# A decay attention and two MLPs on one core: the loads of queries and keys split into 104 and 24 rows, and the whole tokens rebuilt later

## The chip, the core and the metric

The kernel runs on one core of a Trainium2 chip. A core has a matrix engine (TensorE, PE in the profile, with its weight loads as PEld), a vector engine (DVE), a scalar engine (ACT), a general engine (GpSimd, POOL) and a queue engine (SyncE, SP) that here only issues DMA transfers. Each engine runs its own instructions in the order in which they stand and waits on semaphores for the others. The metric is device time in microseconds (us) of one execution.

## The reference

Two batches of eight heads of a decaying linear attention over 768 positions in blocks of 64, then two MLPs, all in float32:

```
rel   = pos[:, None] - pos[None, :]
Dmask = where(rel >= 0, lam ** rel, 0)
for b in range(12):                        # blocks of 64 positions
    intra = ((qb @ kb.T) * Dmask) @ vb
    inter = (qb * lam ** (pos + 1)) @ kv_state
    out[block b] = intra + inter
    kv_state = lam ** 64 * kv_state + (kb * lam ** (63 - pos)).T @ vb
x = out as [1536 tokens, 512]
h = x @ w_in;   x = (h * clip(h + 3, 0, 6) / 6) @ w_out        # first MLP, 2048 wide
h = x @ w_in2;  out = max(0.01 * h, h) @ w_out2                # second MLP
```

## The kernel before

**Attention.** The twelve blocks are the twelve chunks `c` = 0 to 11, both batches and all heads at once. Each chunk has three pieces on PE, 16 small float32 products each: the scores `s` (PSUM tile `pair`, from queries and keys), the state `t` (PSUM tile `a`, from the decayed keys `kd` and the values `vs`) and the output `o` (PSUM tile `h`, from the masked scores `r` and `vs`). Around them ACT copies the queries into `pair` (line 312), so that the state's share comes out of the same products; DVE masks the scores (`r`, line 320); POOL decays the keys (`kd`, line 294); ACT copies the state into the next chunk's `vs` (line 334). The output `o` is the MLP's input: ACT writes its high part `xh` (line 351), DVE the rest `xl` (line 349), and for chunks 0 to 7 ACT also copies the whole value out into `x_spare` (`att_spare`, line 362).

**Loads.** SP issues them in the order of the table `LOAD_ORDER`: a chunk's queries and keys are three loads of 128 rows of 2 KB (`load_qk`, into a ring of four places in `sums`), the values of two chunks two such loads (`load_v`, into `vs`), and two weight slices stand among them (`raw`, two loads each). The helper `load` (line 154) issues them all. Eight semaphores, `DMAHW0` to `DMAHW7`, go round: a load waits until the one eight before it has landed. The other half of a chunk's values is then copied within `vs` by `part_v` (line 287): ACT for chunks 0 to 2, DVE for 3 to 11.

**Borders.** `mm` counts the instruction records that PE gets (four for a float32 product, two for others). The first product at or past record 193 + 256 n + 8 is border n. From the sixteenth load on, six loads at a time wait for a border, through a dependency that `load` adds and that the table `AT_BORDER` repeats for the planner.

**Order.** Nothing is scheduled by hand. Class `Order` plays all operations through a model with a due time and a cost for each, and the order in which they start there is the order of the instructions. `LATENCY`, the costs in the `add` calls and the pieces that wait for a load set it. A change of one number can therefore move instructions on all engines.

**MLPs.** Weights come as 64-bit numbers and are composed to float32 on ACT and DVE (lines 428 to 461: `c`, `t`, `wh`, `wl`), four DVE operations and three ACT ones for a slice and one DVE operation for its low part. Blocks 0 and 1 of the first MLP (four slices of width, three groups of tokens each) use plain products, with a gate on ACT and DVE for each (`u`, `Gh`, `Gl`). From block 2 on, two token groups and two slices are multiplied by seven products instead of eight; these need sums of weights (`s`, line 484) and differences of tokens, T1 to T4, made from `x_spare` (`x_diff`, line 682) and split into high and low parts (line 688 on DVE). `sums_1` orders that work.

```
def load(out, in_):
    i = nc.sync.dma_start(out=out, in_=in_)
    k = (len(loads) - FIRST_LOADS) // LOADS_PER_BLOCK
    loads.append(i)
    if 0 <= k < len(AT_BORDER):
        tc.add_manual_dep(i.ins, borders[...].name, ..., reason="behind the border")
```

Of the kernel before, what the change touches and what calls it, by code (L numbers as in the profile page):

```python
# [9 lines left out]
F32 = mybir.dt.float32  # L10
# [10 lines left out]
DM = H * D  # L21
# [21 lines left out]
FIRST_BORDER, BLOCK, PAST_BORDER = 193, 256, 8  # L43
FIRST_LOADS, LOADS_PER_BLOCK = 15, 6
AT_BORDER = (('o', 0), ('s', 2), ('t', 3), ('s', 5), ('s', 6), ('s', 8), ('o', 8), ('s', 10))
LOAD_ORDER = (('qk', 0), ('v', 0), ('qk', 1), ('qk', 2), ('v', 2), ('qk', 3), ('qk', 4), ('v', 4), ('qk', 5), ('qk', 6), ('v', 6), ('qk', 7), (0, 0, 0), ('qk', 8), ('v', 8), ('qk', 9), ('qk', 10), ('v', 10), (0, 0, 1), ('qk', 11))
# [75 lines left out]
def decay_attention_two_mlps(ctx: ExitStack, tc: tile.TileContext, qkk, vv, lam, w1, w2, out):  # L122
    nc = tc.nc
    eng = {"act": nc.scalar, "dve": nc.vector, "pool": nc.gpsimd}

    sizes = {"raw": 3, "cv": 3, "cl": 2, "w0": 4, "w1": 5, "st": 2, "s": 2, "G": 3, "u": 3, "h": 2, "a": 2, "r": 3, "vs": 3}
    late = {"Gx": 3, "ux": 3}
    const = ctx.enter_context(tc.tile_pool(name="const", bufs=1))
# [23 lines left out]

    def load(out, in_):
        i = nc.sync.dma_start(out=out, in_=in_)  # L154
        k = (len(loads) - FIRST_LOADS) // LOADS_PER_BLOCK
        loads.append(i)
        if 0 <= k < len(AT_BORDER):
            tc.add_manual_dep(i.ins, borders[min(k, len(borders) - 1)].name, mybir.DependencyInfo(
                mybir.DependencyClass.Sync, mybir.DependencyReason.DATA), reason="behind the border")

# [98 lines left out]
    op_warm = add(("pe", T_WARM / 2), lambda _: dense(N_WARM - N_WARM // 2), -800, after=[op_lam])  # L259
    op_a = add(("dve", 1.5), consts_a, -100, takes=["u"] * 3 + ["r"])  # L260
    op_steps = add(("dve", 1.25), consts_b, -100, after=[op_lam, op_a], frees=["h"])
# [5 lines left out]
    def load_qk(c):  # L267
        def fn(_):
            for i in range(3):
                load(QK[c % NQ][:, i], qkk[c, :, i])  # L270
        return fn

    def load_v(c):

        def fn(_):
            vp = new("vs", [P, 2, 2, H, D], F32)
            VS[c], VS[c + 1] = vp[:, 0], vp[:, 1]
            for i in range(2):
                load(vp[:, i, 0], vv[c + i])
            if c == 0:  # L280
                nc.gpsimd.memset(vp[other[1], 0, 1], 0.0)
        return fn
# [70 lines left out]

    SPARE = {}

    def att_spare(c):
        def fn(_):
            j, i = divmod(c, SPT)
            if not i:
                SPARE[j] = pool["s"].tile([P, 2, 2, TT], F32, tag="s", name="x_spare")  # L360
            x = SPARE[j].rearrange("p j k (c b i) -> p (j k) c b i", c=SPT, b=2)[:, :, i]
            nc.scalar.copy(out=x, in_=PA["o", c])
        return fn

    x_ready, spared = {}, {}
    ld = {}
    for c in range(NSC):
        d = due_c[c] - 2.0
        ld["qk", c] = add(("dma", 2.05), load_qk(c), d, takes=["q"])
        ld["vp", c] = ld["vp", c - 1] if c % 2 else add(("dma", 1.4), load_v(c), d if c else 0.0, after=[ld["qk", c]], takes=["vs"])  # L370
        ld["v", c] = add(("act", 0.6 if c else 1.2) if c < 3 else ("dve", 0.5), part_v(c), d - 1.0, after=[ld["vp", c]])
    pieces = {}
    st, copies, masks, dense_ops, att_ops = {}, {-1: []}, [], [op_warm], []
    for c in range(NSC):
        d, last = due_c[c], c + 1 == NSC
        ks = [] if last else [add(("pool", 1.05), k_decay(c, b), d,
                                  after=[ld["qk", c], op_scan[b], st.get(c - 2)]) for b in ((1, 0) if c else (0, 1))]
# [3 lines left out]
        m = add(("dve", 1.13), mask(c), d + 1.2, after=[s, qc, op_const], takes=["r"] if c else [], frees=["pair"])  # L381
        masks.append(m)
        if c < 2:
            op_rows[1 - c] = add(("dve", 1.4), decay_rows(1 - c), d + 4.0, after=[m])
# [12 lines left out]
        x_ready[c] = add(("dve", 0.69), att_x(c, True), d + 5.0, after=[hi])  # L397
        if c < 2 * SPT:
            spared[c] = add(("act", 0.58), att_spare(c), d + 5.0, after=[hi], takes=["s"] * (not c % SPT))
        add(("none", 0.0), nothing, after=[x_ready[c], spared.get(c)], frees=["h"])  # L400
        att_ops += [x_ready[c], m, o, *ks, *copies.get(c, []), *([st[c]] if c in st else [])]
# [13 lines left out]
    def load_w(h):  # L415
        def fn(_):
            l, f, j = h
            RAW[h] = new("raw", [P, DM, 2], U32)
            raw, w = RAW[h].rearrange("p n t -> p (n t)"), (w1, w2)[l][f, j].bitcast(U32)
            for a in (slice(0, DM), slice(DM, 2 * DM)) if l + f < 2 else (slice(0, 2 * DM),):  # L420
                (load if h in LOAD_ORDER else nc.sync.dma_start)(raw[:, a], w[:, a])
        return fn
# [63 lines left out]

    composed, low = {}, {}
    for l in range(2):
        for f in range(NF):
# [11 lines left out]
            if paired(l, f) and f % 2:  # L501
                p, i = f // 2, None
                for n in range(4):
                    i = add(("dve", 0.43), w_sum(l, p, n), after=[composed[l, f - 1, 0], composed[l, f, 0], i])
                hi = add(("act", 1.05), s_high(l, p), after=[i], takes=["s"])
                s_ready[l, p] = add(("dve", 1.22), s_low(l, p), after=[hi], frees=["raw"])
                add(("none", 0.0), nothing, after=[i, low[l, f - 1, 0], low[l, f, 0]], frees=["cv"] * 2)
# [144 lines left out]

    XT, CS = {}, {}
    A_B = (("A11", "B11"), ("S1", "T1"), ("S2", "T2"), ("A12", "B21"), ("S3", "T3"), ("S4", "B22"), ("A22", "T4"))
# [22 lines left out]
    def spare(k, n):  # L677
        i = {"B11": 0, "T1": 0, "B21": 1, "T4": 1, "B12": 2, "T3": 2, "B22": 3, "T2": 3}[n]
        return SPARE[i // 2][:, i % 2]

# [3 lines left out]
    def x_split(k, n, lo, src):  # L684
        def fn(_):
            xh, xl = XT[k, n]
            if lo:
                nc.vector.tensor_tensor(out=xl, in0=src(k, n), in1=xh.bitcast(F32), op=ALU.subtract)
            else:
                nc.scalar.copy(out=xh, in_=src(k, n))  # L690
        return fn

# [280 lines left out]

    def sums_1():
        u = ("dve", 1.22)
        for n, t in (("B11", 0), ("B21", 0), ("B22", 1)):
            x_op[0, 0, n] = x_of(PAIR[t])
        t1 = add(u, x_diff(0, "T1", "B12", "B11", spare), after=list(spared.values()))
        t3 = add(u, x_diff(0, "T3", "B22", "B12", spare), after=[t1])
        t2 = add(u, x_diff(0, "T2", "B22", "T1", spare), after=[t3])  # L980
        t4 = add(u, x_diff(0, "T4", "B21", "T2", spare), after=[t2])
        for n, after in (("T1", [t2]), ("T2", [t4]), ("T4", [t4]), ("T3", [t3, last1[0, PAIR[1]]])):
            splits(0, 0, n, [op_late, *after], spare)
        done = [x_op[0, 0, n][0] for n in ("T1", "T4", "T3", "T2")]
        for d in (done[:2], done[2:]):
            add(("none", 0.0), nothing, after=d, frees=["s"])
# [72 lines left out]

    sums_1()  # L1060
    for b in range(SINGLE, len(BLOCKS[0])):
# [45 lines left out]
```

## Time and profile before

| | us |
|---|---|
| median of 3 runs | 563.14 |
| lowest and highest of them | 562.85, 564.15 |
| the profiled execution, whole time | 563.63 |
| its span, first to last instruction | 561.9 |
| PE busy | 548.5 (98% of the span) |
| DVE busy | 411.9 |
| ACT busy | 362.3 |

The span is what the profile shows; 1.7 us of the profiled execution's time lie around it. Matmuls are pipelined, so a busy PE may still be late. Idle time of an engine matters only where the last one to finish waits for it.

### The profile page before, as it was taken

What the parts mean: (1) busy time and instruction counts of PE and PEld (TensorE: products, weight loads), DVE (VectorE), ACT (ScalarE), POOL (GpSimd) and SP (SyncE); (2) the same over time, 40 slices, a digit from 0 to 9 for tenths busy, and PEclk for the clock granted to TensorE, in tenths of its full rate; (3) what the DMA queues carried; (4) which work ended last, traced back from release to release, by engine and by line L of the source; (5) the groups of instructions that cost most, each with busy time, mean ns of one, the idle gap of its engine ahead of it and who ended that gap; (6) DMA issues with size and microseconds to landing.
All of it is one profiled execution on the core that took longest, in us unless ns stands there. A gap on an engine that the chain in (4) does not pass through costs nothing.

```text
span 561.9 us, 9098 instructions
## 1 busy us (share of the span) xinstructions
PE 548.5 (98%) x3512; PEld 458.2 (82%) x3512; DVE 411.9 (73%) x690; ACT 362.3 (64%) x634; POOL 67.5 (12%) x77
## 2 busy tenths in 40 slices
PE   8888999999999999999999999999999999999996
PEld 5877888888788888888888888888888888888885
DVE  7879999987987974787689897686368943782342
ACT  5988895667666745578676886687268825683220
POOL 7651001101111101101000000000110110110000
PEclk9999999999999999999999999999999999999999
DMA  8984334534447433534200402241434622512332
GB/s 312 315 296 172 113 112 94 128 116 113 86 109 190 115 84 75 130 114 93 76 1 1 157 31 80 71 150 38 94 81 124 168 56 43 132 42 50 75 73 77
DMA packets 25596, 61.66 MB, mean 110 GB/s; under 512 B 3026, under 2 KB 3282, under 8 KB 25554
## 3 DMA queue, kind: packets, MB, share of 16 engines
q1 hardware_dynamic: 18672, 48.77, 26.8%
q0 software_dynamic: 6480, 11.80, 12.3%
q8 instruction: 27, 0.44, 0.4%
q10 hardware_dynamic: 402, 0.52, 0.3%
q14 instruction: 15, 0.12, 0.1%
HBM read 46.14 MB, written 3.15 MB: 88 GB/s over the span
## 4 chain that ended last, share of the span: by engine, by line
PE 90%; DVE 4%; DMA 2%; ACT 1%; issue 1%; POOL 1%; SPq 0%; DVEq 0%; POOLq 0%; ACTq 0%
PE acc L148 44%; PE h L148 27%; PE a L148 18%; DMA sums<-st 1%; DVE r L320 1%; DMA vs<-vv 1%; PE pair L148 1%; POOL kd L294 1%; DVE vs L287 1%; DVE t L441 0%; DVE u L550 0%; DVE t L451 0%; SPq L154 0%; DVE decay L242 0%; DVE Gl L563 0%
## 5 line engine op out<-in xcount | busy, mean ns | idle before, releaser
L580 POOL DMA_DIRECT2D sums<-st x45 | 39.5, 926 | 426.0 <-ACT st L636 426.0
L148 PE MATMUL acc<-Gl,wh 128*128 128x512 f32 x136 | 53.1, 390 | 0.1
L148 PE MATMUL acc<-Gh,wh 128*128 128x512 f32 x136 | 53.1, 390 | 0.0
L148 PE MATMUL acc<-Gh,wl 128*128 128x512 f32 x136 | 53.0, 390 | 0.0
L148 PE MATMUL acc<-wl,Gh 128*128 128x512 f32 (+1 forms) x128 | 49.6, 388 | 0.0
L148 PE MATMUL acc<-wh,Gh 128*128 128x512 f32 (+1 forms) x128 | 49.6, 387 | 0.0
L148 PE MATMUL acc<-wh,Gl 128*128 128x512 f32 (+1 forms) x128 | 49.5, 387 | 0.0
L451 DVE CUSTOM_DVE_ANT_0 t<-t,c 128x1024 uint16<-128x1024 uint16 x64 | 45.0, 704 | 2.2
L636 ACT COPY st<-acc 128x512 f32<-128x512 f32 x43 | 25.1, 587 | 32.1 <-PE acc L148 15.9
L428 ACT ACTIVATE c<-raw 128x512 uint32<-128x512 uint32 x64 | 42.7, 669 | 4.7 <-DVE t L451 3.1
L449 DVE SCALAR_TENSOR_TENSOR t<-raw,t 128x512 uint32<-128x512 uint32 x64 | 44.1, 688 | 1.1
L457 ACT CAST wh<-t 128x512 fp32r<-128x512 f32 (+1 forms) x64 | 37.7, 593 | 9.1 <-DVE t L451 6.2
L432 ACT ACTIVATE t<-raw 128x512 f32<-128x512 f32 x64 | 42.6, 667 | 0.0
L461 DVE TENSOR_TENSOR wl<-t,wh 128x512 fp32r<-128x512 f32 (+1 forms) x64 | 41.2, 652 | 0.7 <-ACT wh L457 0.4
L148 PE MATMUL a<-xh,wh 128*128 128x512 f32 (+1 forms) x108 | 38.9, 360 | 0.0
L566 DVE TENSOR_TENSOR Gl<-u,Gh 128x512 fp32r<-128x512 f32 x32 | 22.1, 689 | 22.9 <-ACT Gh L754 22.7
L148 PE MATMUL h<-xh,s 128*128 128x512 f32 x112 | 38.7, 390 | 0.0
L148 PE MATMUL a<-xh,wl 128*128 128x512 f32 (+1 forms) x108 | 38.7, 358 | 0.0
L148 PE MATMUL a<-xl,wh 128*128 128x512 f32 (+1 forms) x108 | 38.7, 358 | 0.0
L638 DVE TENSOR_TENSOR sums<-acc,sums 128x512 f32<-128x512 f32 x26 | 17.9, 690 | 28.0 <-PE acc L148 28.0
L438 DVE TENSOR_SCALAR t<-t 128x512 f32<-128x512 f32 x64 | 27.0, 422 | 15.3 <-ACT t L432 15.2
L760 ACT ACTIVATE u<-a 128x512 f32<-128x512 f32 x24 | 14.3, 597 | 25.8 <-PE a L148 25.8
(176 smaller groups left out, 1447.2 us busy)
## 6 DMA issues: line engine op xcount, KB each, us to landing
raw<-w SPq DMA_DIRECT2D x58, 512.0 KB, 3.3
sums<-st POOLq DMA_DIRECT2D x45, 256.0 KB, 4.1
sums<-qkk SPq DMA_DIRECT2D x36, 256.0 KB, 4.9
vs<-vv SPq DMA_DIRECT2D x12, 256.0 KB, 5.1
raw<-w SPq DMA_DIRECT2D x12, 256.0 KB, 4.1
out<-sums SPq DMA_DIRECT2D x19, 128.0 KB, 2.3
out<-sums ACTq DMA_DIRECT2D x3, 128.0 KB, 2.7
out<-sums SPq DMA_DIRECT2D x2, 64.0 KB, 2.3
```

The lines of the kernel that those rows point to most:

```text
L148: i = nc.tensor.matmul(out, a, x, **flags)
L428: nc.scalar.activation(out=CV[h][1], in_=RAW[h][:, :, 0], func=AF.Copy, scale=2.0 ** -29)
L432: return lambda _: nc.scalar.activation(out=CV[h][0].bitcast(F32), in_=RAW[h][:, :, 1].bitcast(F32), func=AF.Abs)
L438: nc.vector.tensor_scalar(out=t.bitcast(F32), in0=t.bitcast(F32), scalar1=MAG_MIN, scalar2=MAG_MAX, op0=ALU.max, op1=ALU.min)
L449: nc.vector.scalar_tensor_tensor(out=t, in0=RAW[h][:, :, 1], scalar=0xC0000000, in1=t, op0=ALU.bitwise_and, op1=ALU.bitwise_or)
L451: nc.vector.tensor_tensor(out=t, in0=t, in1=c, op=ALU.add)
L457: nc.scalar.copy(out=W[h][0][:, cols(*h)], in_=CV[h][0].bitcast(F32)[:, cols(*h)])
L461: return lambda e: eng[e].tensor_tensor(out=W[h][1][:, cols(*h)], in0=CV[h][0].bitcast(F32)[:, cols(*h)], in1=W[h][0].bitcast(F32)[:, cols ...
L566: nc.vector.tensor_tensor(out=gl, in0=U[s], in1=gh.bitcast(F32), op=ALU.subtract)
L580: return lambda _: nc.gpsimd.dma_start(out=SUM[t][:, e, :], in_=STAGE[t, e], accum_op=ALU.add)
L636: nc.scalar.copy(out=STAGE[t, e], in_=ps)
L638: nc.vector.tensor_tensor(out=acc, in0=ps, in1=acc, op=ALU.add)
```

## The change

All queries' and keys' loads from chunk 3 on are issued as two loads, of rows 0 to 103 and of rows 104 to 127; values and weights stay at 128 rows. `FIRST_LOADS` is 99, more than there are loads in the table, so no load waits for a border. Within a chunk the second and third load change places: the keys for `kd` come before the keys for the scores. `part_v` goes to ACT for the odd chunks from 3 on. `att_spare` is gone; instead `x_whole` adds `xh` and `xl` on DVE, four operations of 128x1024, once the attention is done, and `s` takes the attention's memory. Some costs and the DMA latency of the planner have other numbers, so that the order moves everywhere until about a third of the way through the program.

```diff
-LATENCY = {"dma": 2.0, "pe": 0.15, "act": 0.15, "dve": 0.15, "pool": 0.15}
+LATENCY = {"dma": 2.5, "pe": 0.15, "act": 0.15, "dve": 0.15, "pool": 0.15}
-FIRST_LOADS, LOADS_PER_BLOCK = 15, 6
+FIRST_LOADS, LOADS_PER_BLOCK = 99, 6
+FEWER = (slice(0, 104), slice(104, 128))
+FEWER_FROM, FEWER_QK, FEWER_V, FEWER_RAW = 3, (0, 1, 2), (), ()
-    def load(out, in_):
-        i = nc.sync.dma_start(out=out, in_=in_)
+    def load(out, in_, fewer=False):
         k = (len(loads) - FIRST_LOADS) // LOADS_PER_BLOCK
-        loads.append(i)
-        if 0 <= k < len(AT_BORDER):
+        loads.append(k)
+        for p in FEWER if fewer else (slice(0, P),):
+            i = nc.sync.dma_start(out=out[p], in_=in_[p])
+            if 0 <= k < len(AT_BORDER):
...
-            for i in range(3):
-                load(QK[c % NQ][:, i], qkk[c, :, i])
+            for i in (0, 2, 1):
+                load(QK[c % NQ][:, i], qkk[c, :, i], c >= FEWER_FROM and i in FEWER_QK)
...
-        ld["v", c] = add(("act", 0.6 if c else 1.2) if c < 3 else ("dve", 0.5), ...)
+        ld["v", c] = add(("act", 0.6 if c else 1.2) if c < 3 else ("act", 0.6) if c % 2 else ("dve", 0.8), ...)
...
-        if c < 2 * SPT:
-            spared[c] = add(("act", 0.58), att_spare(c), d + 5.0, after=[hi], takes=["s"] * (not c % SPT))
...
+    def x_whole(k, n):
+        def fn(_):
+            if n == "B11" or n == "B22" and not k:
+                SPARE[k, int(n == "B22")] = pool["s"].tile([P, 2 << k, 2, TT >> k], F32, ...)
+            x = [part([x[i].bitcast(F32) for x in X], k, n) for i in range(2)]
+            nc.vector.tensor_tensor(out=spare(k, n), in0=x[0], in1=x[1], op=ALU.add)
+        return fn
...
+        for n, t in (("B11", 0), ("B12", 1), ("B22", 1), ("B21", 0)):
+            w[n] = last_whole[0] = add(u, x_whole(k, n), after=[op_late, last_whole.get(0), *x_of(ts[t])],
+                                       takes=["s"] * (n == "B11" or n == "B22" and not k))
```

How the change moves instructions is shown at three places. First SP: `sums` is the ring of queries and keys, `vs` the values. From the third load of chunk 3 to the values of chunk 5 there stood before:

```order
L154 DMA sums<-qkk 128x512 [waits DMAHW0_49,PE_49]
L154 DMA sums<-qkk 128x512 [waits DMAHW1_49]
L154 DMA sums<-qkk 128x512 [waits DMAHW2_49]
L154 DMA sums<-qkk 128x512 [waits DMAHW3_49,Pool_49]
L154 DMA vs<-vv 128x512 [waits DMAHW4_49]
L154 DMA vs<-vv 128x512 [waits DMAHW5_49]
```

Now, chunk 4 and the values of chunks 4 and 5:

```order
L159 DMA sums<-qkk 104x512 [waits DMAHW4_49,PE_49]
L159 DMA sums<-qkk 24x512 [waits DMAHW5_49]
L159 DMA sums<-qkk 104x512 [waits DMAHW6_49,Pool_49]
L159 DMA sums<-qkk 24x512 [waits DMAHW7_49]
L159 DMA sums<-qkk 104x512 [waits DMAHW0_49]
L159 DMA sums<-qkk 24x512 [waits DMAHW1_49]
L159 DMA vs<-vv 128x512 [waits DMAHW2_49]
L159 DMA vs<-vv 128x512 [waits DMAHW3_49]
```

A chunk's three loads are six issues, each with its turn of the eight semaphores; the wait for PE at the third load of chunk 3 was a border, the one left is the ring's place coming free.

Second DVE, the masks and the copies of values in the middle of the attention (`pair` and `r` are scores before and after the mask, `xl0` the low part of the output for the first group of tokens). Before:

```order
L287 COPY vs_319<-vs_319 64x512 x2
L320 TENSOR_TENSOR r_414<-pair_364,decay_106 128x1024
L349 TENSOR_TENSOR xl0_111<-h_397,xh0_110 128x4x128
L349 TENSOR_TENSOR xl0_111<-h_436,xh0_110 128x4x128
L320 TENSOR_TENSOR r_502<-pair_394,decay_106 128x1024
L287 COPY vs_453<-vs_453 64x512 x2
L320 TENSOR_TENSOR r_549<-pair_499,decay_106 128x1024
```

Now, from the copy for chunk 8 to the first weight slice (`t_613`):

```order
L290 COPY vs_563<-vs_563 64x512
L352 TENSOR_TENSOR xl1_110<-h_616,xh1_109 128x4x128
L323 TENSOR_TENSOR r_682<-pair_584,decay_103 128x1024
L430 TENSOR_SCALAR t_613<-t_613 128x512
L433 TENSOR_SCALAR t_613<-t_613 128x512
L441 SCALAR_TENSOR_TENSOR t_613<-raw_491,t_613 128x512
L443 ISA t_613<-t_613,c_614 128x1024
```

Two copies in a row ahead of a mask have become one; the copy for chunk 8 now stands ahead of the mask of chunk 7 and of the first weight slice.

Third PE, the last pieces ahead of the first weight product (`pair` are scores, `a` states, `h` with `r` outputs, `h` with `wh` the MLP). Before:

```order
L148 MATMUL pair_659<-sums_109 64x64 x16
L148 MATMUL a_709<-vs_453,kd1_108 64x64 x16
L148 MATMUL h_735<-r_684,vs_453 64x64 x16
L148 MATMUL a_764<-vs_574,kd0_107 64x64 x16
L148 MATMUL h_789<-r_732,vs_574 64x64 x16
L148 MATMUL pair_785<-sums_109 64x64 x16
L148 MATMUL a_839<-vs_574,kd1_108 64x64 x16
L148 MATMUL h_861<-xh0_110,wh_811 128x512
```

Now:

```order
L150 MATMUL pair_757<-sums_106 64x64 x16
L150 MATMUL a_805<-vs_563,kd0_104 64x64 x16
L150 MATMUL h_832<-r_779,vs_563 64x64 x16
L150 MATMUL pair_829<-sums_106 64x64 x16
L150 MATMUL a_872<-vs_563,kd1_105 64x64 x16
L150 MATMUL h_895<-xh0_107,wh_822 128x512
```

The scores have moved up by one place: ahead of the first weight product now stand those of chunk 10 too, and between a chunk's state and its output the scores of a later chunk.

## Rows read from the trace of the kernel before

**Rows 1.** Windows: stretch, length, busy us (instructions) of each engine, clock, DMA.

```profile
0.00:46.00 46.00, 38.41 (x943) 31.74 (x944) 37.41 (x50) 35.68 (x63) 28.01 (x32) 1.00 0.91 310
...
60.00:130.00 70.00, 70.00 (x310) 57.95 (x310) 64.31 (x108) 53.16 (x91) 5.39 (x6) 1.00 0.39 111
130.00:520.00 390.00, 388.70 (x1827) 324.70 (x1826) 282.10 (x490) 253.07 (x446) 34.08 (x39) 1.00 0.35 90
```

**Rows 2.** Waits of PE, 9.1 to 46.1 us: us in total, times, longest.

```profile
PE h L148 <- DVE r L320: 2.2, 3, 0.9
PE a L148 <- POOL kd L294: 1.9, 2, 1.2
PE pair L148 <- issue: 0.9, 1, 0.9
PE a L148 <- ACT vs L334: 0.5, 2, 0.3
PE pair L148 <- ACT pair L312: 0.5, 2, 0.2
PE a L148 <- issue: 0.2, 1, 0.2
```

**Rows 3.** Timeline of PE, 44 to 47 us: start, us, operation, idle before it.

```profile
44.54 0.30 PE L148 MATMUL a<-vs,kd 128*64 128x64 f32 x2 [1.23 <-POOL kd L294]
45.10 1.15 PE L148 MATMUL a<-vs,kd 128*64 128x64 f32 x30 [0.26 <-ACT vs L334]
46.17 0.50 PE L148 MATMUL h<-xh,wh 128*128 128x512 f32 x1
```

**Rows 4.** Timelines of DVE and ACT on the way to it, 38 to 45 us.

```profile
38.19 1.22 DVE L320 TENSOR_TENSOR r<-pair,decay 128x1024 f32<-128x1024 f32 x1
...
43.22 0.62 ACT L457 CAST wh<-t 128x512 fp32r<-128x512 f32 x1 [1.11 <-DVE t L451]
```

**Rows 5.** Waits of SP's queue, 5 to 42 us.

```profile
SPq L154 <- PE pair L148: 7.4, 4, 3.7
SPq L154 <- PE h L148: 2.1, 1, 2.1
```

**Rows 6.** DMA, 5 to 46 us: packets, MB, share of 16 engines.

```profile
q1 hardware_dynamic: 7228, 13.21, 93.2%
q8 instruction: 7, 0.11, 1.2%
```

**Rows 7.** Window 38.3 to 39.8 us: SP's timeline and the instruction queue.

```profile
38.34 1.43 SPq L154 DMA_DIRECT2D raw<-w  x1
...
q8 instruction: 1, 0.02, 3.9%
```

**Rows 8.** SP's issues: timeline; line 650's stores (ns, min/median/max); `qkk` loads.

```profile
7.93 0.99 SPq L154 DMA_DIRECT2D sums<-qkk  x2
...
24.43 0.90 SPq L154 DMA_DIRECT2D raw<-w  x2
...
L650 SPq DMA_DIRECT2D out<-sums x21: 466/549/603, 523.5 to 557.9; - x21
...
DMA to landing us min/median/max: 2.7/4.9/5.7
```

**Rows 9.** Timelines of POOL and DVE, 16 to 21 us.

```profile
16.08 4.53 POOL L294 TENSOR_TENSOR kd<-sums,decay 64x512 f32<-64x512 f32 x4 [1.80 <-DMA sums<-qkk]
...
18.59 2.31 DVE L287 COPY vs<-vs 64x512 f32<-64x512 f32 x2
```

**Rows 10.** Lines, 5 to 46 us: count, busy us, mean ns of one, idle before.

```profile
L287 DVE COPY vs<-vs 64x512 f32<-64x512 f32 x9 | 7.0, 799 | 0.2
...
L362 ACT COPY x_spare<-h 128x512 f32<-128x512 f32 x8 | 4.7, 586 | 0.0
```

**Rows 11.** Timelines of DVE and PE at the first pair of slices.

```profile
100.16 1.22 DVE L484 TENSOR_TENSOR s<-raw,s 128x1024 fp32r<-128x1024 f32 x1
...
111.74 0.39 PE L148 MATMUL h<-T10h,s 128*128 128x512 f32 x1
```

More of the change, by code (lines that the diff above doesn't have):

```diff
@@ L151, in mm @@
         records[0] += 4 if a.dtype == F32 else 2
-    def load(out, in_):
-        i = nc.sync.dma_start(out=out, in_=in_)
+    def load(out, in_, fewer=False):
         k = (len(loads) - FIRST_LOADS) // LOADS_PER_BLOCK
-        loads.append(i)
-        if 0 <= k < len(AT_BORDER):
-            tc.add_manual_dep(i.ins, borders[min(k, len(borders) - 1)].name, mybir.DependencyInfo(
-                mybir.DependencyClass.Sync, mybir.DependencyReason.DATA), reason="behind the border")
+        loads.append(k)
+        for p in FEWER if fewer else (slice(0, P),):
+            i = nc.sync.dma_start(out=out[p], in_=in_[p])
+            if 0 <= k < len(AT_BORDER):
+                tc.add_manual_dep(i.ins, borders[min(k, len(borders) - 1)].name, mybir.DependencyInfo(
+                    mybir.DependencyClass.Sync, mybir.DependencyReason.DATA), reason="behind the border")
     starts = [[sum(bs[:i]) for i in range(len(bs) + 1)] for bs in BLOCKS]
@@ L278, in fn @@
             for i in range(2):
-                load(vp[:, i, 0], vv[c + i])
+                load(vp[:, i, 0], vv[c + i], c >= FEWER_FROM and i in FEWER_V)
             if c == 0:
@@ L352, in att_x @@
         return fn
[L354 to L365, printed above, removed]
+    x_ready = {}
     ld = {}
@@ L380, in decay_attention_two_mlps @@
         s = pieces["s", c] = add(pe, scores(c), d, after=[qc, op_warm])
-        m = add(("dve", 1.13), mask(c), d + 1.2, after=[s, qc, op_const], takes=["r"] if c else [], frees=["pair"])
+        m = add(("dve", 1.22 if c else 1.4), mask(c), d + 1.2, after=[s, qc, op_const], takes=["r"] if c else [], frees=["pair"])
         masks.append(m)
         if c < 2:
-            op_rows[1 - c] = add(("dve", 1.4), decay_rows(1 - c), d + 4.0, after=[m])
+            op_rows[1 - c] = add(("dve", 2.1), decay_rows(1 - c), d + 4.0, after=[m])
         add(("none", 0.0), nothing, after=[s, qc] + ks, frees=["q"])
@@ L419, in fn @@
             raw, w = RAW[h].rearrange("p n t -> p (n t)"), (w1, w2)[l][f, j].bitcast(U32)
-            for a in (slice(0, DM), slice(DM, 2 * DM)) if l + f < 2 else (slice(0, 2 * DM),):
-                (load if h in LOAD_ORDER else nc.sync.dma_start)(raw[:, a], w[:, a])
+            for i, a in enumerate((slice(0, DM), slice(DM, 2 * DM)) if l + f < 2 else (slice(0, 2 * DM),)):
+                if h in LOAD_ORDER:
+                    load(raw[:, a], w[:, a], i in FEWER_RAW)
+                else:
+                    nc.sync.dma_start(out=raw[:, a], in_=w[:, a])
         return fn
@@ L972, in splits, with sums_1 @@
         x_op[l, k, n] = [add(("dve", 0.61 * u), x_split(k, n, True, src), after=[hi])]
-    def sums_1():
-        u = ("dve", 1.22)
+    last_whole = {}
+    def sums_1(k):
+        u, ts = ("dve", 0.61 * (2 - k)), (2, 2) if k else PAIR
         for n, t in (("B11", 0), ("B21", 0), ("B22", 1)):
[L977 to L985, printed above, removed]
+            x_op[0, k, n] = x_of(ts[t])
+        w = {}
+        for n, t in (("B11", 0), ("B12", 1), ("B22", 1), ("B21", 0)):
+            w[n] = last_whole[0] = add(u, x_whole(k, n), after=[op_late, last_whole.get(0), *x_of(ts[t])],
+                                       takes=["s"] * (n == "B11" or n == "B22" and not k))
+        t1 = add(u, x_diff(k, "T1", "B12", "B11", spare), after=[w["B11"], w["B12"]])
+        t3 = add(u, x_diff(k, "T3", "B22", "B12", spare), after=[t1, w["B22"]])
+        t2 = add(u, x_diff(k, "T2", "B22", "T1", spare), after=[t3])
+        t4 = add(u, x_diff(k, "T4", "B21", "T2", spare), after=[t2, w["B21"]])
+        for n, after in (("T1", [t2]), ("T2", [t4]), ("T4", [t4]), ("T3", [t3, last1[0, ts[1]]])):
+            splits(0, k, n, after, spare)
+        done = [x_op[0, k, n][0] for n in ("T1", "T3", "T2", "T4")]
+        for d in (done,) if k else (done[:2], done[2:]):
             add(("none", 0.0), nothing, after=d, frees=["s"])
@@ L1058, in block @@
         seconds(l, b)
-    sums_1()
+    sums_1(0)
+    od.ops[s_at[0, starts[0][SINGLE] // 2]][3].append(last_whole[0])
     for b in range(SINGLE, len(BLOCKS[0])):
```

26 lines of the change are left out of this document (13 added, 13 removed).

## The prediction, made before the changed kernel had run

> **What bounds the kernel now.** I read the windows first. From 60 to 130 us PE is busy for 70.00 of 70 us, from 130 to 520 for 388.70 of 390; in the first 46 us for 38.41 [rows 1]. Behind the attention PE is dense and does the same products in either kernel, so time can only be won before 46 us, or lost by putting a wait into the dense part. What the first part loses is told by PE's waits between 9.1 and 46.1 us: 2.2 + 1.9 + 0.9 + 0.5 + 0.5 + 0.2 = 6.2 us [rows 2]. Of the 1.9 put down to POOL, 1.2 is the wait that ends at 44.54; the other 0.7 is at the first state, which the change leaves alone. So 5.5 us are in reach.
>
> Who is behind them is seen one step further back. The wait at 44.54 is put down to POOL, but the ACT copies of the state, which the same product needs, stand behind the cast `wh`, and that waited 1.11 us for the weight's last DVE step [rows 3, 4]: ACT's order, not POOL. The masks `r` come late where copies of values stand before them on DVE: two copies took 2.31 us while POOL was busy from 16.08 to 20.6 [rows 9]; the nine average 799 ns [rows 10]. "Issue" is PE without an instruction: 1.1 us in all [rows 2]. Under all this the loads run nearly without a break: 13.21 MB from 5 to 46 us at 93.2% of the sixteen engines [rows 6], with SP standing 7.4 + 2.1 us at PE's pieces, most of it at borders [rows 5].
>
> **The change, part by part.**
>
> *Borders go, loads are split.* A 256 KB load costs 0.932 x 41 x 0.262 / 13.21 = 0.76 us of all engines [rows 6]. The issue costs SP 0.47 from one to the next (two in 0.90, of which the second is 0.43) [rows 8]. Split, a load takes two issues, 0.94 us or more, so SP sets the pace and not the engines, if the bytes cost what they cost now. No row shows a load of 104 or 24 rows. Bounds for one such step: 0.47, as for whole loads, and 0.63, a little over the slowest store of 64 rows (0.603) [rows 8]. I take 0.53: the direction is that of the loads, the shape is not. The far bound for the engines is that 24 rows cost a whole load, 1.52 us for a pair; I don't take it, since the bytes are the same, but it stays in the tail. The Trainium skill, "DMA: Bandwidth & Descriptors", section "Why a DMA increments its semaphore by 16 and not by 1", says that a transfer uses the largest number of engines up to 16 that divides its rows, the lowest-numbered ones: 13 for 104 rows, 12 for 24; by its count, as an estimate, the busiest engine would carry ten rows instead of eight, 0.95 us a load in place of 0.76, and the sum by it would be the same, because two issues at 0.53 are longer.
>
> Now the path. Chunk 3's six issues start at 7.93 [rows 8] and each waits for a whole load ahead of it to land, at the 0.76 of such a load: 12.5. From there to the first value load of chunk 8 stand 30 halves and 6 whole loads: 30 x 0.53 + 6 x 0.47 = 18.7, issue at 31.2, landed 2.7 later (the least that a load takes here [rows 8]; with half the bytes in flight I take the least): 33.9. Behind its landing DVE has, in the new order, the copy (0.8), `xl` (0.7), the mask of chunk 7 and the four steps of the first weight slice, then ACT `wh`, two copies of queries and those of the state, then PE the last state and the first weight product. From that mask's start to that product it is 46.17 - 38.19 = 8.0 us now [rows 3, 4], without the queries' copies, which are 1.2 at the 0.59 of an ACT copy of 128x512 [rows 10]. So the load path allows the first weight product at 33.9 + 0.8 + 0.7 + 8.0 + 1.2 = 44.6; at 0.47 a step 42.8, at 0.63 47.6.
>
> *Order of PE.* The first weight product now starts at 46.17 with chunk 10's scores still to do, 1.1 us; in the new order they lie ahead of it. The mark to compare with is 47.3.
>
> *PE's waits, one by one.* Issue, 1.1: I take it as gone, bounds 0 and 1.1, since halves let an instruction packet pass sooner. Masks, 2.2 in three: the copies of the odd chunks leave DVE and another piece stands between; I take 1.5 of it away, bounds 0 and 2.2. The wait at 44.54 and the 0.26 behind it: the cast still stands ahead of the state copies on ACT, so they stay. The rest, ACT's, 1.0 less that 0.26: stays. Against it, scores stand one place earlier than now, so a late load stops an output as well; I take the 0.5 of the row "ACT pair" [rows 2] once more as its price, bounds 0 and 1.0. Sum: -1.1 - 1.5 + 0.5 = -2.1, first weight product at 45.2. The load path allows that up to a step of 0.55.
>
> *ACT and POOL.* Eight copies to `x_spare` leave ACT, 4.7 us; copies of values for five odd chunks come, five operations at no more than the 586 ns of those copies, 2.9 [rows 10]. Net -1.8 on an engine that waits for PE and is waited for; I count nothing of its own for it. POOL's work stays; its keys come second instead of third.
>
> *Whole tokens on DVE.* Four additions of 128x1024, at 1.22 (the price of the operation of that size in rows 11), 4.9 us behind the attention; and two of the four differences, 2.4, which DVE now does during the attention, come there too: 7.3 us in all. From 60 to 130 us DVE is busy for 64.31 of 70 [rows 1], so this has to come out of a lead: the weight sum `s` is done at 101.4 and first used at 111.74 [rows 11], 10.3 us. 10.3 - 7.3 = 3.0 us stay, and more, since in the new order 19 more products stand between the first weight product and that use. Counted at nothing; without that cover each addition would cost up to 1.22.
>
> Sum against the profiled execution: 563.63 - 2.1 = 561.5. The median is 0.5 below that execution, so I say 561.0.
>
> **The rivals.**
>
> *A. The instruction packets still collide; slower.* Seven packets of 16 KB came from 5 to 46 us [rows 6]. In the stretch of one of them a load's issue took 1.43 us instead of 0.43 [rows 7]; it is one of five such issues between 13 and 40 us. If the split does not keep them apart, four fall before chunk 8's values: four times 1.0, first weight product 44.6 + 4.0 = 48.6, 1.3 later than the mark. And with nothing held back at the borders PE waits for its instructions more often: the longest such wait now is 0.9; six times would be 5.4 in place of 1.1, half of that increase 2.2. Together +3.5, 566.6. It decides from the point where more than half of the packets meet a full queue. For it: SP's waits at the borders, 9.5 us, are what thins the queue today. Against it: half as many bytes are in flight in eight issues. The same page of the Trainium skill would leave the three highest engines free of queries and keys; the trace doesn't say on which engine the packets ran, so by that rule the clash goes or stays whole.
>
> *B. Halves cost like the stores.* At 0.63 a step the load path gives 47.6, 0.3 behind the mark: 563.4, no change. The far bound of the engines (1.52 for a pair in place of 1.06, fifteen pairs) would put it at 44.6 + 6.9 = 51.5, and the time at 567.3.
>
> *C. DVE late behind the attention.* The additions stand among the gates; if PE waits for half of each, 4 x 0.6 = 2.4, the gain is gone: 563.4. Against it the lead of 3.0 us or more.
>
> **How the numbers follow.** Forecast 0.50 (its own range 559.1 to 562.0), A 0.17, B 0.18 at 563.4 and 0.05 at its far end, C 0.07, and 0.03 that nearly all of the 5.5 us go (557.6). Faster by over 0.2% (1.1 us, about what a measurement here can tell from no change): 0.50 + 0.03 = 0.53. Slower: 0.17 + 0.05 = 0.22. Within: 0.25. The range leaves out the 0.03 at the bottom and the upper half of A with B's far end, about 0.15: 558.8 to 565.6.
>
> **What would show it.** In the trace of the changed kernel: the step from one half load's issue to the next (0.53; B if 0.6 or more); no load issue over 1 us beside an instruction packet (A if there are still five); PE's waits on issue near 0 and on `r` under 1 us; the first weight product at 45.2 or before, with chunk 10's scores ahead of it; the first product with T1 without a wait, and PE dense from there to 520 us. I am wrong if the first weight product is not earlier than 46, or if it is and the dense part has new waits on DVE.

## The result: 570.5 us, slower by 1.3%

The changed kernel takes 570.50 us (median of 6 runs, 569.91 to 572.14) where the kernel before takes 563.57 (6 runs beside it). The ratio is 1.0127, its 95% interval 1.0108 to 1.0146. The forecast was 561.0, its range 558.8 to 565.6: wrong in sign and outside the range.

The profiled execution took 570.76 us with a span of 569.0, against 563.63 and 561.9 before: 7.1 us more. The page's first line and the same windows as [rows 1] say where; the last line is the stretch from 46 to 60 us before, which [rows 1] leaves out:

```profile
PE 550.9 (97%) x3512; PEld 461.0 (81%) x3512; DVE 411.5 (72%) x689; ACT 360.8 (63%) x631; POOL 67.5 (12%) x77
```

```profile
0.00:46.00 46.00, 35.80 (x845) 30.03 (x847) 28.95 (x41) 31.75 (x55) 25.91 (x30) 0.96 0.87 259
46.00:60.00 14.00, 11.68 (x258) 10.10 (x255) 10.03 (x15) 10.61 (x19) 2.18 (x2) 0.97 0.81 246
60.00:130.00 70.00, 70.00 (x353) 57.90 (x350) 63.58 (x100) 50.20 (x85) 5.36 (x6) 0.98 0.34 91
130.00:520.00 390.00, 388.80 (x1827) 324.86 (x1826) 292.01 (x508) 258.43 (x456) 34.01 (x39) 1.00 0.37 94
```

```profile
46.00:60.00 14.00, 14.00 (x230) 11.71 (x225) 13.83 (x21) 12.68 (x23) 0.00 (x0) 1.00 0.27 91
```

From 60 us on PE is as dense as before. The four additions, 4.9 us on DVE, all lie between 60 and 130 us and nobody waits for them; that DVE is busy for 292.01 instead of 282.10 us in the last window is work on weights and gates that comes later than before. Up to 60 us PE does 2.6 us less in the first window than before (35.80 against 38.41) and stands 2.3 us in the second, where it stood for none. PE's busy time grew too, from 548.5 to 550.9, for as many products (x3512), and the granted clock is lower in the first three windows: I put 2.4 of the 7.1 us down to the clock, and 4.7 are idle time (569.0 - 550.9 = 18.1 against 561.9 - 548.5 = 13.4).

PE's waits from 9.1 to 50 us, to be read against [rows 2], and the largest one behind:

```profile
PE a L150 <- ACT vs L337: 2.1, 2, 1.9
PE pair L150 <- DMA sums<-qkk: 1.9, 2, 1.2
PE pair L150 <- ACT vs L337: 1.2, 1, 1.2
PE h L150 <- issue: 1.1, 1, 1.1
PE a L150 <- issue: 1.1, 1, 1.1
...
PE h L150 <- DVE u L542: 2.2, 1, 2.2
```

The waits on the masks and on POOL are gone. In their place PE waits for loads: directly (`pair` on `qkk`), and through ACT, which was itself late for its values. The first weight product, which [rows 3] had at 46.17 with one more piece behind it, comes at 50.85 (PE's timeline):

```profile
49.30 0.97 PE L150 MATMUL a<-vs,kd 128*64 128x64 f32 x25
50.44 0.45 PE L150 MATMUL a<-vs,kd 128*64 128x64 f32 x7 [0.17 <-issue]
50.85 0.47 PE L150 MATMUL h<-xh,wh 128*128 128x512 f32 x1
```

SP's timeline and its waits from 5 to 50 us show the pace of the loads, and DVE's timeline when the values of chunk 8 came; the last row is the DMA queue from 5 to 46 us, which answers to [rows 6]:

```profile
12.67 3.53 SPq L159 DMA_DIRECT2D sums<-qkk  x6
16.77 0.83 SPq L159 DMA_DIRECT2D vs<-vv  x2
17.82 6.97 SPq L159 DMA_DIRECT2D sums<-qkk  x12
24.99 0.83 SPq L159 DMA_DIRECT2D vs<-vv  x2
26.16 3.03 SPq L159 DMA_DIRECT2D sums<-qkk  x6
29.24 1.56 SPq L159 DMA_DIRECT2D raw<-w  x2
31.90 4.28 SPq L159 DMA_DIRECT2D sums<-qkk  x6
36.29 0.83 SPq L159 DMA_DIRECT2D vs<-vv  x2
```

```profile
SPq L159 <- DMA sums<-qkk: 10.7, 23, 1.0
SPq L159 <- DMA vs<-vv: 2.3, 5, 0.6
```

```profile
39.53 0.42 DVE L290 COPY vs<-vs 64x512 f32<-64x512 f32 x1 [4.95 <-DMA vs<-vv]
```

```profile
q1 hardware_dynamic: 6249, 10.98, 88.8%
```

Twelve halves, six loads' worth, take 24.99 - 17.82 = 7.17 us: 1.20 a pair. Before, six whole loads took 4.76 from their first issue to that of the values, 0.79 each:

```profile
16.47 3.92 SPq L154 DMA_DIRECT2D sums<-qkk  x6
21.23 0.80 SPq L154 DMA_DIRECT2D vs<-vv  x2
```

SP no longer stands at borders; it stands 13.0 us at loads that have not landed, half a microsecond at a time. So 10.98 MB came in the stretch that had brought 13.21, although the packets' times still add up to 88.8% of the engines' time: 0.888 x 41 x 0.262 / 10.98 = 0.87 us of all sixteen a load, where it was 0.76.

### The profile page after: what moved, and what is told of

Same layout as the page of the kernel before. It is cut to its first block, busy times and chain, and to the rows that moved or that the text cites. A ratio compares the mean times of both kernels' runs of the same rounds, so it can differ in the third digit from the quotient of the medians.

```text
span 569.0 us, 9134 instructions
## 1 busy us (share of the span) xinstructions
PE 550.9 (97%) x3512; PEld 461.0 (81%) x3512; DVE 411.5 (72%) x689; ACT 360.8 (63%) x631; POOL 67.5 (12%) x77
## 3 DMA queue, kind: packets, MB, share of 16 engines
q0 software_dynamic: 6480, 11.80, 12.2%
## 4 chain that ended last, share of the span: by engine, by line
PE 89%; DMA 8%; SPq 1%; ACT 1%; issue 0%; DVE 0%; DVEq 0%; ACTq 0%
PE acc L150 45%; PE h L150 26%; PE a L150 17%; DMA sums<-qkk 6%; SPq L159 1%; DMA raw<-w 1%; PE pair L150 0%; ACT pair L315 0%; ACT vs L337 0%; DVE a L736 0%; DVE u L542 0%; ACT u L538 0%; ACT t L424 0%; ACT vs L290 0%; DVE sums L598 0%
## 5 line engine op out<-in xcount | busy, mean ns | idle before, releaser
L555 DVE SCALAR_TENSOR_TENSOR Gl<-u,Gh 128x512 fp32r<-128x512 f32 x36 | 24.6, 686 | 9.3 <-ACT Gh L548 9.2
```

The lines of the kernel that those rows point to most:

```text
L555: nc.vector.scalar_tensor_tensor(out=gl, in0=U[s], scalar=1.0 / 6.0, in1=gh.bitcast(F32), op0=ALU.mult, op1=ALU.subtract)
```

## The experiments

Each is run beside the kernel before; ratios are against that. The first four ask whether it is the loads at all, and what in them. The theories E, L and O that they set against each other are stated with the first. Times are medians; the rows come from one profiled execution each, which for the splits into 64, 96 and 120 rows and for one load of three was the fastest of its kernel.

**All loads whole, still without borders** (a_whole). The order of the attention is that of the changed kernel; behind the attention it shifts a little.

```diff
-FEWER_FROM, FEWER_QK, FEWER_V, FEWER_RAW = 3, (0, 1, 2), (), ()
+FEWER_FROM, FEWER_QK, FEWER_V, FEWER_RAW = 99, (0, 1, 2), (), ()
```

> The changed kernel with all loads at 128 rows and still no borders (the order of the attention is that of the changed kernel; behind the attention the planner's order shifts a little). In the changed kernel the loads bring 10.98 MB from 5 to 46 us instead of 13.21, the values of chunk 8 are issued at 36.3 instead of 28.1, and the first weight product starts at 50.85 instead of 46.17. Theory E, the shapes 104 and 24 use 13 and 12 of the 16 engines: with whole loads the bytes come back to 13 MB or more, first weight product at 44.5 to 46.5, time 561 to 564.5. Theory L, eight semaphores of halves allow only half the bytes under way: the same here. Theory O, the new order of ACT, DVE and PE is what costs: first weight product still at 49 or later, time 568 or more.

565.24 us, ratio 1.0022 (1.0007 to 1.0037). The split alone costs 570.5 - 565.2 = 5.3 us, so theory O's time falls. E and L get their bytes, 13.73 MB from 5 to 46 us, but their range was missed by 0.7, and the first weight product stands where O had it (PE's timeline):

```profile
49.44 0.50 PE L150 MATMUL h<-xh,wh 128*128 128x512 f32 x1
```

So only 1.4 of the 5.3 us stand at that product (50.85 against 49.44); the rest of what the split costs comes behind it. What is left of the loss without the split is on other rows, PE's waits up to 62 us:

```profile
PE pair L150 <- issue: 3.9, 2, 2.5
PE h L150 <- issue: 1.7, 1, 1.7
PE a L150 <- DVE kd L252: 0.6, 1, 0.6
PE a L150 <- issue: 0.5, 1, 0.5
```

PE waits for no load any more, but 6.1 us for its own instructions, all of it before 50 us.

**Two halves of 64 rows** (a_64), as many issues and bytes as 104 and 24.

```diff
-FEWER = (slice(0, 104), slice(104, 128))
+FEWER = (slice(0, 64), slice(64, 128))
```

> The changed kernel with its loads split in two halves of 64 rows in place of 104 and 24: as many issues, as many bytes in a pair, the same order on PE, DVE, ACT and POOL. Theory E (rows of 104 and 24 leave three and four engines idle): 64 rows use all 16, the bytes from 5 to 46 us come back to 12.5 MB or more, first weight product at 46.5 or earlier, time 561 to 565. Theory L (the eight semaphores are turned round with half the bytes each): as slow as the changed kernel, 11 MB, 569 to 571.5. Theory O: 568 or more.

572.67 us, 1.0157 (1.0138 to 1.0176): slower still, which theory E excluded. SP's timeline, the durations of its `qkk` issues (ns, min/median/max) and its largest wait:

```profile
18.64 8.73 SPq L159 DMA_DIRECT2D sums<-qkk  x12
27.47 1.01 SPq L159 DMA_DIRECT2D vs<-vv  x2
```

```profile
L159 SPq DMA_DIRECT2D sums<-qkk x63: 328/587/1487, 0.7 to 54.1; - x63
```

```profile
SPq L159 <- DMA vs<-vv: 2.2, 4, 0.8
```

Here it is the issue: 587 ns each, 1.47 us a pair, with SP hardly waiting for landings (3.7 us in all). That is rival B's mechanism, for this shape and at a higher price: 0.74 from one issue to the next where B had 0.63. It does not settle L either: SP was not held by its eight semaphores.

**120 and 8 rows** (a_120).

```diff
-FEWER = (slice(0, 104), slice(104, 128))
+FEWER = (slice(0, 120), slice(120, 128))
```

> The changed kernel with its loads split into 120 and 8 rows: the same order on PE, DVE, ACT and POOL, as many issues. Theory E: 120 rows on 15 engines with 8 rows each, 8 rows on 8 engines with one each, so the busiest engine carries 9 rows a pair where 104 and 24 give it 10 and whole loads 8: between the two, 564 to 568, and most of the time 15 packets under way at once where the changed kernel has 13. Theory L: as slow as the changed kernel, 569 to 571.5.

569.89 us, 1.0101 (1.0073 to 1.0128): E's range was missed by 1.9, L's was met; but the profiled execution took 566.88, inside E's range, and 15 packets under way, as E had it, are the most frequent number there (table below). Its twelve halves take 7.15 us, as long as with 104 and 24, and SP waits 12.2 us for landings. Its issues are the cheapest of all, median 324 ns.

**The kernel before without borders** (b_nodep), its order unchanged on all engines.

```diff
-        if 0 <= k < len(AT_BORDER):
+        if False:
             tc.add_manual_dep(i.ins, ...)
```

> The kernel before with its order on every engine and its whole loads, but no load waits for a border. Theory E says nothing of this. If the borders only cost (my prediction's premise), the loads end earlier and the time falls by 0.5 to 2 us, to 561.5 to 563. If the borders protect PE's instruction packets from a full queue, PE's waits on issue grow from 1.1 us to 3 or more and the time is 565 or more.

563.69 us, 1.0001 (0.9990 to 1.0012). The first weight product stands at 46.82, no earlier than in [rows 3]. Loads came sooner (13.67 MB), PE's waits on masks and POOL shrank from 4.1 to 1.3 us, but its waits on issue rose from 1.1 to 3.2. So in this order the borders neither cost nor give: what the loads gain without them PE loses on issue. My premise that they hold the attention back was wrong.

**Whole loads with borders** (a_border): what remains is all of the change but the split.

```diff
-FIRST_LOADS, LOADS_PER_BLOCK = 99, 6
+FIRST_LOADS, LOADS_PER_BLOCK = 15, 6
-FEWER_FROM, ... = 3, (0, 1, 2), (), ()
+FEWER_FROM, ... = 99, (0, 1, 2), (), ()
```

> The changed kernel with whole loads and with the borders of the kernel before (sixteenth load on, six at a time): what is left of the change is the order of the loads in a chunk, the copies of values on ACT, the whole tokens behind the attention and the planner's numbers. Whole loads without borders took 565.24, with PE waiting 6.1 us for instructions up to 50 us. If that wait comes from the full queue, the borders bring it to 2.5 us or less and the time to 560.5 to 563. If it is the new order that costs, it stays at 564 to 566.

562.78 us, 0.9977 (0.9954 to 1.0001): 2.5 us under whole loads without borders. In the new order, then, borders are worth something. By which wait stays open: the profiled execution was the slowest of ten (565.25), and in it PE waited 5.0 us on issue, against 6.1 without borders, 2.8 of them at once, with the window behind it:

```profile
22.96 0.97 PE L150 MATMUL pair<-sums 64*64 64x64 f32 x25 [2.79 <-issue]
```

```profile
20.00:24.00 4.00, 1.21 (x34) 1.00 (x32) 0.36 (x1) 2.37 (x4) 0.03 (x1) 1.00 0.58 209
24.00:28.00 4.00, 4.00 (x84) 3.88 (x84) 2.07 (x3) 2.00 (x4) 2.11 (x2) 0.57 0.77 224
```

That such waits are for instruction packets the traces do show. I counted PE's records (products and weight loads) in the order of their start, in all fourteen traces up to 62 us. Of 29 waits on issue of 0.4 us or more 27 end at record 193 + 256 n or the one behind it, the numbers from which the kernel counts its borders, and 1.2 to 1.6 us after a packet of 16 KB of the instruction queue has ended. The wait of 2.79 us ends at record 706; the packet ahead of it took 2.34 us. The two others end at record 1348, one of them in the changed kernel.

**96 and 32 rows** (a_96).

```diff
-FEWER = (slice(0, 104), slice(104, 128))
+FEWER = (slice(0, 96), slice(96, 128))
```

> The changed kernel with its loads split into 96 and 32 rows: both are multiples of 16 rows, as 64 and 64, where the issue of 64 rows took 0.59 us and SP stood at its own issues; the orders on PE, DVE, ACT and POOL are those of the changed kernel. If the issue of a half on all 16 engines costs 0.59 whatever its rows: 570 to 573, SP waiting little for landings. If only the number of busy engines and the packets' time count, issues of 0.45 or less, packets mostly at 84 ns and 563 to 566. If small loads as such stretch the packets: packets over 100 ns, 567 to 571.

570.38 us, 1.0110 (1.0081 to 1.0139). Its twelve halves take 8.35 us, issue median 420 ns, SP's waits for landings from 5 to 50 us 8.1 us; 41% of its packets took 100 ns or more, 53% stand at 84. No reading of the three fits whole: the time lies in the ranges of the first and the last, the issue is the second's. In the twelve halves' stretch (17.92 to 26.27) the issues take 6.6 of the 8.35 us, two of them 1.48 and 1.30, landings hold SP for 1.1, and the DMA share is 0.76 where the changed kernel's stretch has 0.93. So for this shape it is mostly the issues, as with 64 rows, and not full engines.

**One load of three split** (a_one).

```diff
-FEWER_FROM, FEWER_QK, FEWER_V, FEWER_RAW = 3, (0, 1, 2), (), ()
+FEWER_FROM, FEWER_QK, FEWER_V, FEWER_RAW = 3, (1,), (), ()
```

> The changed kernel with only one of a chunk's three loads split (the keys for the scores), the other two whole: a third of the halves. If the loss is the loads' pace, it goes with the number of halves: between whole loads (565.2) and the changed kernel (570.5), nearer to the first: 565.5 to 568. If a few halves already break the stream, 569 or more. If fewer bytes under way spare PE's instruction packets without costing pace, 562 to 565.

567.42 us, 1.0057 (1.0035 to 1.0079). A third of the splits brings 2.2 of the 5.3 us: the loss goes roughly with their number. Its DMA row, 5 to 46 us:

```profile
q1 hardware_dynamic: 6852, 12.34, 101.0%
```

The packets' times add up to more than the engines' whole time and yet they move less than whole loads did in 95.3% (13.73 MB). So packets became longer, which the next one shows without any small load.

**The 24 rows left out** (a_only104).

```diff
-FEWER_FROM, ... = 3, (0, 1, 2), (), ()
+FEWER_FROM, ... = 4, (0, 1, 2), (), ()
-        for p in FEWER if fewer else (slice(0, P),):
+        for p in FEWER[:1] if fewer else (slice(0, P),):
```

> The changed kernel with the loads of 24 rows left out from chunk 4 on, so that rows 104 to 127 of queries and keys keep the contents of four chunks earlier: 13 busy engines and no small load. If the small loads stretch the packets, these go back to 84 ns for most packets, with 13 under way at once, 0.67 to 0.75 us from one landing to the next. If 13 engines are slower for each packet, the packets stay at 100 to 120 ns and a load takes 0.85 us or more.

568.18 us in one run. Packet times were not restored, so the small loads are not what stretches them. Nor does the slower pace need theory L: without a half, six loads of 208 KB take 5.46 us, 0.91 each, where whole loads of 256 KB took 0.79, and SP waits for landings in 3.2 of these 5.46 us:

```profile
13.75 4.88 SPq L159 DMA_DIRECT2D sums<-qkk  x6
19.21 1.35 SPq L159 DMA_DIRECT2D vs<-vv  x2
```

The time itself says less, because PE also waited 8.6 us on issue in this run. Counted from the packet records of each trace, packets of 2 KB that began from 12 to 44 us:

```
                         packets   at 80-90 ns   100 ns or more   most often under way at once
before, 128                 4826       92%            5%               16
a_whole, 128                5141       87%            4%               16
changed, 104 + 24           3893       29%           60%               13
a_only104, 104              4072       25%           64%               13
a_all104, values too        3610       43%           48%               13
a_120, 120 + 8              3995       43%           50%               15
a_96, 96 + 32               3849       53%           41%               16
a_64, 64 + 64               3540       70%           26%               16
a_one, a third split        4383       30%           58%               16
```

(With 120 and 8 rows, 16 are under way nearly as long as 15.)

**Halves by columns** (a_col), two loads of 128 rows with half a row each.

```diff
-        for p in FEWER if fewer else (slice(0, P),):
-            i = nc.sync.dma_start(out=out[p], in_=in_[p])
+        for p in (slice(0, 4), slice(4, 8)) if fewer else (slice(None),):
+            i = nc.sync.dma_start(out=out[:, p] if fewer else out, in_=in_[:, p] if fewer else in_)
```

> The changed kernel with each of its split loads cut by columns: two loads of 128 rows with 256 elements each, so that both halves use as many engines as a whole load and bring half a row each; the orders on PE, DVE, ACT and POOL are those of the changed kernel. If an issue on all engines costs what the rows cost (0.43 to 0.47 for 128 rows), SP sets the pace with 0.9 to 0.94 us a pair: 565 to 568, and SP waits little for landings. If halves as such lose the pace: 569 or more. If only the uneven use of engines in 104 and 24 cost: packets at one value for nearly all, 564 to 566.

567.10 us, 1.0068 (1.0045 to 1.0091), within the first reading: most of its packets of 1 KB take 46 ns, so nothing is stretched, and 89% of its 2 KB ones take 80 to 90. SP sets the pace:

```profile
16.96 7.14 SPq L159 DMA_DIRECT2D sums<-qkk  x12
24.20 0.86 SPq L159 DMA_DIRECT2D vs<-vv  x2
```

1.21 a pair at a median of 422 ns an issue, two of the twelve at 1.27 and 1.04; from 5 to 50 us SP waits 4.8 us for landings and 4.3 for PE and POOL. In this stretch the pace is that of the changed kernel, and yet the time is 3.4 us less: over the whole attention it falls behind by less, and the values of chunk 8 are issued at 33.04 instead of 36.29.

**The values split as well** (a_all104).

```diff
-FEWER_FROM, FEWER_QK, FEWER_V, FEWER_RAW = 3, (0, 1, 2), (), ()
+FEWER_FROM, FEWER_QK, FEWER_V, FEWER_RAW = 3, (0, 1, 2), (0, 1), ()
```

> The changed kernel with the values from chunk 4 on also split into 104 and 24 rows, so that almost no load of 128 rows is left among the halves. If the packets are stretched because loads of 128 and of 104 rows stand in the engines' queues together, most of them go back to 84 ns, with 13 under way. If 104 rows stretch them by themselves, the median stays at 100 ns or more. Either way fewer engines carry more: 570 to 574.

571.51 us in one run; 13 packets under way, 43% of them at 84 ns. Mixing 128 and 104 rows is thus part of it at most.

**The whole tokens alone** (c_tok): the changed kernel with the loads and their order, the borders, the copies of values and the planner's numbers of before.

```diff
...
-FIRST_LOADS, LOADS_PER_BLOCK = 99, 6
+FIRST_LOADS, LOADS_PER_BLOCK = 15, 6
...
-FEWER_FROM, ... = 3, (0, 1, 2), (), ()
+FEWER_FROM, ... = 99, (0, 1, 2), (), ()
...
-            for i in (0, 2, 1):
+            for i in range(3):
...
-... if c < 3 else ("act", 0.6) if c % 2 else ("dve", 0.8), part_v(c), ...
+... if c < 3 else ("dve", 0.5), part_v(c), ...
...
```

> The whole tokens behind the attention alone: the loads, the borders, the copies of values and the planner's numbers of the kernel before, but no copies to x_spare, and the four additions with the differences behind the attention. If the additions stay behind other work, as my prediction says, there is no wait of PE on the differences or on T1 to T4, and the time is 562.3 to 563.8, within 0.2% of before. If DVE is late behind the attention, PE waits at T1 to T4 and the time is 564.5 or more. If ACT was the bound of the attention, the 4.7 us it gives up show as 1 to 2 us less: 561 to 562.3.

562.15 us (12 runs), 0.9979 (0.9963 to 0.9995): of the parts tried alone the only one that gains. It lies just under the first reading's range and in the last one's. All of PE's waits from 60 to 520 us:

```profile
PE a L150 <- DVE a L736: 1.2, 2, 0.6
```

The kernel before has the same wait, with the same numbers. No wait on the additions, the differences or T1 to T4: rival C has no row. Whether the gain comes from ACT's time, as the last reading has it, is not shown, and it is at the limit of what can be told. Up to 50 us PE's waits on the masks are 0.2 us here instead of 2.2, those on issue 4.5 instead of 1.1.

**The copies of values alone** (c_v), in the kernel before.

```diff
-... if c < 3 else ("dve", 0.5), part_v(c), ...
+... if c < 3 else ("act", 0.6) if c % 2 else ("dve", 0.8), part_v(c), ...
```

> The kernel before with the copies of values of the odd chunks from 3 on moved from DVE to ACT, alone. If masks behind two copies cost, as I read it, PE's wait on r (2.2 us) falls under 1 and the time by 0.5 to 1.5 us, to 561.8 to 562.8. If ACT, which the state copies need, pays for it: 563.5 to 565.

563.97 us, 1.0007 (0.9996 to 1.0017): no change that can be told, and PE's waits on the masks did not fall but rose:

```profile
PE h L148 <- DVE r L320: 3.5, 8, 0.9
```

The order of the loads within a chunk and the planner's numbers were not tried alone.

## Why the prediction was wrong

**The step that failed** is "SP sets the pace and not the engines, if the bytes cost what they cost now". The condition did not hold. I priced 30 halves and 6 whole loads at 18.7 us; from 12.67 (I had 12.5) to 36.29 they took 23.6, 2.8 more on the halves (18.7 for 15.9) and 2.1 more on the whole loads among them (4.9 for 2.8). The issues themselves were cheaper than my lower bound of 0.47 (line of the `qkk` loads, ns min/median/max):

```profile
L159 SPq DMA_DIRECT2D sums<-qkk x63: 298/365/1352, 0.8 to 49.9; - x63
```

The 4.9 us are landings: between 12.67 and 36.29 SP waited 7.2 us for loads, where my sum had none, and saved about 2.9 on the issues. My price of an issue was too high, and the bytes' price I had taken from whole loads.

**The engines.** What I left in the tail, as the far bound of rival B, was the right direction with too large a size for a pair: 1.52 us there, 1.20 measured (and the 567.3 that it gave was still too small, because the sum ended at the first weight product). Two things add up, both in the table. Most often only 13 packets are under way at once. The Trainium skill's page "DMA: Bandwidth & Descriptors", section "Why a DMA increments its semaphore by 16 and not by 1", gives 13 engines for 104 rows, and the trace agrees with its 13 packets under way. By that page of the Trainium skill alone, as the prediction estimated, a pair would have taken 0.95 us. The packets' mean rose from 95 to 113 ns, 60% of them taking 100 or more in place of 84; an estimate with that 0.95, 0.95 x 113 / 95 = 1.13 us, comes near the 1.20, and one from the traces alone, 0.76 x 16 / 13 x 113 / 95 = 1.11 us, does too. Why the packets are longer is not settled. It is not the small load (a_only104), not the number of engines alone (a_96, with 16 under way), not the mixing of 104 and 128 alone (a_all104), and not halves as such (a_col). Whole loads and halves by columns, in which every load spreads its 128 rows alike, are the shapes without it. That the eight semaphores, holding fewer bytes, add a part of their own (theory L) is not excluded.

**The path was right in kind, and its number in part by luck.** Put the landing as it was, 39.53, in place of my 33.9, and the same sum gives 39.53 + 0.8 + 0.7 + 8.0 + 1.2 = 50.2 for the first weight product; it came at 50.85. The landing took 3.2 us, not 2.7. But the last wait of any length before that product was for another load, the keys of chunk 9, for which I had 0.5 us in all (PE's timeline):

```profile
45.13 1.15 PE L150 MATMUL pair<-sums 64*64 64x64 f32 x32 [1.17 <-DMA sums<-qkk]
```

From there PE ran dense to 50.85, but for 0.17; the chain from the values of chunk 8 over DVE and ACT was done just as early, its state copies at 49.11 for a piece that PE began at 49.30. Against the mark of 47.3 that is 3.5 us lost. Whole loads in the same order lose 2.1 there as well, to waits on issue.

Over the kernels of this order without borders that ran more than once, the time goes roughly with the issue of chunk 8's values (us, from SP's timelines): whole loads 26.10 and 565.2, a_one 31.00 and 567.4, a_col 33.04 and 567.1, a_120 35.26 and 569.9, a_96 35.59 and 570.4, the changed kernel 36.29 and 570.5, a_64 38.58 and 572.7.

**What came on top.** The second weight slice was late for the same reason, and ACT waited for it:

```profile
52.38 0.67 ACT L420 ACTIVATE c<-raw 128x512 uint32<-128x512 uint32 x1 [2.78 <-DMA raw<-w]
```

The gate of the first slice stands behind that on ACT and DVE, an output of the attention waits for the gate, and PE stood 2.16 us. And twice the granted clock fell behind PE's longest waits (1.86 us up to 31.79, 2.16 up to 58.17), to means of 0.61 and 0.69 over 4 us: with levels of 2.4 and 1.2 GHz the lower one for most of these 4 us. PE's timeline and windows:

```profile
31.79 2.37 PE L150 MATMUL a<-vs,kd 128*64 128x64 f32 x31 [1.86 <-ACT vs L337]
...
58.17 1.29 PE L150 MATMUL h<-r,vs 128*64 128x64 f32 x32 [2.16 <-DVE u L542]
```

```profile
28.00:32.00 4.00, 2.05 (x58) 1.83 (x54) 2.70 (x3) 1.53 (x3) 2.00 (x2) 0.97 0.91 278
32.00:36.00 4.00, 3.94 (x78) 3.68 (x79) 2.04 (x3) 1.89 (x4) 1.52 (x2) 0.61 0.88 238
...
56.00:60.00 4.00, 1.84 (x45) 1.72 (x46) 2.49 (x4) 3.89 (x8) 0.00 (x0) 0.88 0.53 192
60.00:64.00 4.00, 4.00 (x35) 3.38 (x32) 3.21 (x5) 2.89 (x6) 0.00 (x0) 0.69 0.00 0
```

No wait of the kernel before was over 1.3 us in this part and its clock stayed at 1.00, so this had no place in my sum. The first fall lies before the first weight product and is contained in the 3.5; with 2.2 for the gate and, as an estimate, 0.5 + 1.2 for the second fall (0.12 and 0.31 of 4 us, some of which PE stood idle) that makes 7.4, against 7.1. Whole loads had neither this wait nor a fall of the clock behind 49.44, so this is where most of the split's 5.3 us lie, and my sum, which ended at the first weight product, had it at nothing.

**PE's waits.** On the masks I took 1.5 of 2.2 away: all went, but with PE late everywhere that says little. c_v shows that moving the copies of values does not do it, and in c_tok, which leaves them on DVE, the waits went all the same: my reading that these copies make the masks late is not borne out. On issue I took 1.1 as gone, since halves would let an instruction packet pass sooner; 2.2 stood there up to 50 us, and no run shows such a gain from halves. The 0.5 for late loads was 1.9, and 3.3 more through ACT's state copies.

**Rival A** (0.17) had the sign and a wrong place. In the changed kernel issue is the smaller part, one of its two long waits ends at an instruction packet's record, and of the five load issues over 1 us between 13 and 40 us two are left. It shows in whole loads without borders, 6.1 us of such waits, all four at those records.

**The whole tokens** cost nothing, as forecast; alone they gain about 1.2 us, which I had counted at nothing.

## What to carry to other kernels

A DMA's price has two sides, the issue and the bytes, and a new shape changes both: 84 ns a packet in a full queue was measured here with whole loads, and every split by rows moved away from it (26 to 60% of packets at 100 ns or more), so such a split has to be priced as unknown on the engines, not only on the issuing queue. Late loads cost behind the mark as well as before it, and a long wait of PE may be paid twice, since the clock may fall behind it. Test a bundle part by part: here the one part that gained alone was buried under another that cost four times as much.

## What the runs showed that I had not expected

- The time of an issue does not go in the order of size: `qkk` issues have medians of 324 ns (120 and 8 rows), 365 (104 and 24), 420 (96 and 32), 587 (64 and 64). Nor is it the shape's alone: whole loads have 404 in the kernel before and 328 in a_whole, and in a_96's twelve halves an issue right behind another took 423 to 427 ns, one behind a wait 311 to 372, apart from the two slow ones.
- Packets of 2 KB went from 84 ns to 100 and more as soon as a third of the loads was split by rows, with packet times at 101% of the engines' time.
- The clock does not fall behind every long wait: with the whole tokens alone PE waited 2.46 us up to 31.43, and the windows from 28 to 36 us stand at 1.00.
- Nearly all long waits of PE on issue end at records 256 apart, behind instruction packets, as counted under a_border.
